# A fused pooled-attention and MLP kernel: q of batch 1 cast by GpSimd's load, w2's last quarters issued sooner, group 0's output units ahead of group 1's hidden pairs

## The chip, the core and the metric

The kernel runs on one core of a Trainium2 chip. A core has five engines with their own instruction streams: TensorE (PE in the profile, with PEld for its weight loads), VectorE (DVE), ScalarE (ACT), GpSimd (POOL) and SyncE (SP), which here only issues transfers. All operands lie in SBUF, a memory of 128 partitions; TensorE writes to PSUM, eight banks of 512 float32 per partition, from which VectorE and ScalarE copy results. Transfers run on 16 DMA engines that the queues share: q1 holds SP's transfers, q10 ScalarE's, q0 GpSimd's. Only GpSimd's queue changes the type of the data on the way.

The metric is the time of one launch on the device in microseconds (us), as the median of several runs.

## What is computed

Eight batches of eight heads, 576 positions, 64 values per head. Keys and values are averaged over blocks of 8 positions (72 pooled positions); each query attends to these. The result, 4608 rows of 512, goes through a two-layer MLP with the gate h - tanh(h).

```python
k_p = k.reshape(B, H, Sp, pool, D).mean(axis=3)      # Sp = 72
v_p = v.reshape(B, H, Sp, pool, D).mean(axis=3)
scores = scale * np.matmul(q, k_p.transpose(0, 1, 3, 2))
attn = softmax(scores)
x = np.matmul(attn, v_p)            # then to (4608, 512)
h = x @ w_in                        # 512 -> 2048
g = h - np.tanh(h)
out = g @ w_out                     # 2048 -> 512
```

## The kernel before

The first 512 positions of each batch b make group b of the MLP (NG = 9 groups of 512 rows; the ninth collects the last 64 positions of all batches). The order of all work is written out by hand, in one program order from which each engine takes its own instructions; the framework adds the waits. While TensorE works on one group's MLP, the other engines load and prepare the next batch.

**Group 0** is special, because attention of batches 0 and 1 and the loads of both weight matrices share its time. `mlp_h_mms` (L577) and `mlp_h_act` (L588, L590) compute its 16 blocks of h. Its output product is made of 16 *units*: `mlp_o(0, tb, qd, gts)` (L605) multiplies row block tb by quarter qd of w2, four matmuls of 512 columns. `W2_ORDER = (0, 8, 4, 12)`: the quarters are the rows 0 to 3, 8 to 11, 4 to 7 and 12 to 15 of w2b, in blocks of 128, each loaded by one `load_w2` (L757) on GpSimd's queue, which casts to 16 bits. The round of units with qd 3 ends with copies into O (L614 by VectorE, L616 by ScalarE) and the stores. The text calls the units of one qd a *round*.

Between the units stands attention of batch 1: pooling of k (`pool_k`, L248 to L259), its transposition (`k_transpose`, L341, with copies into KB on VectorE), the casts of q to 16 bits (`q1_cast` L979, tail L1009), the turn of q by TensorE (`q_pe_transpose` L216, `q_pe_tail` L228, evacuated at L132 or L134), the scores (`scores_wide`, `scores_ends`, L387) and their exponentials on ScalarE (L402, L419, L420), v's pooling (`pool_v1`, L292, L312), the product with v (`av_mms` L476, division L511 and L512) and the turn of the result (`turn1`, L555, evacuated at L562 into xT). These use PSUM banks 4 to 7 in turn, counted by `ps_a`; the units hold banks 0 to 3.

**Groups 1 to 8** use another scheme: seven products of half size in place of eight (one step of Strassen's algorithm in Winograd's form). For it, sums of w2's quarters are prepared once in w2s: `w_sum` (L663) fills w2s[0], [1], [2] on VectorE and w2s[3] on GpSimd, `negated` (L988) fills w2s[4] on ScalarE, and b12 is replaced by b22 - b12 in place. A group's h comes from `h_pair` (L623 on TensorE, tanh at L636 on ScalarE, difference at L637 on VectorE into Gt), seven pairs and two single blocks; VectorE also makes the sums P, Q and the differences Dg (L645, L650, L655). Then follow 14 half products (`product`, L680) with the next batch's scores (`head_scores`, L435) and attention (L461) between them.

In group 1 of the kernel before, one unit of the last round stands behind the second pair (p == 1), and the other three stand in `rest_of_group_0()`, ahead of the fifth pair (p == 4), with the casts and DMA transposes of batch 2's q, the second half of w2s[2], and the difference in b12.

**Loads around the change.** GpSimd issues v of batch 0, four parts of w1, and w2's quarters qd 0 and qd 1 in a row at the start. The quarters qd 2 and 3 are issued after pool_k(1); qd 2 waits until qd 1 has landed, and qd 3 stands behind two parts of w2s[3]. SP issues k of batch 1 (once w1's second part has landed), then q of batch 1 (L172), then v of batch 1 (L138); ScalarE issues the tail of q (L164). A DMA issue also waits for the earlier transfer that had its semaphore.

Of the kernel before, what the change touches and what calls it, by code (L numbers as in the profile page):

```python
# [9 lines left out]
BF16 = mybir.dt.bfloat16  # L10
F16 = mybir.dt.float16
ACT = mybir.ActivationFunctionType
ALU = mybir.AluOpType
# [7 lines left out]
R = 4  # L21
QA = 128 * R
# [7 lines left out]
NT = 5  # L30
# [13 lines left out]
def kernel(  # L44
# [74 lines left out]

    q_raws = {}  # L120
# [104 lines left out]
    def q_pe_tail(b):  # L225
        ps = ps_any([128, NHP, QT], FP32, "qt_ps")
        for hp in range(NHP):
            nc.tensor.matmul(  # L228
                ps[:, hp, :],
                lhsT=q_bf[:, R, 2 * hp : 2 * hp + 2, :].rearrange("p h d -> p (h d)"),  # L230
                rhs=ident[:, 0:QT],
                start=True,
                stop=True,
            )
        evac(q_tiles(b)[1][:, :, :], ps[:, :, :])

    def halves(n, b):
        return ((0, n),) if b < 2 else ((0, n // 2), (n // 2, n))

    def pool_k(b, eng, t0=0, t1=NT, last=None, parts=(0, 1)):  # L240
        r = k_raw[b % 2].rearrange("p t (j d) -> p t j d", d=D)[:, t0:t1, :, :]
        if b not in kdups:
            kdups[b] = work.tile([128, NT, 2, D], BF16, name="kd", tag="kd", bufs=1)
        kd = kdups[b][:, t0:t1, :, :]
        n = t1 - t0
        if 0 in parts:
            for ta, tb in halves(n, b):
                eng.tensor_tensor(  # L248
                    out=r[:, ta:tb, 0:4, :],
                    in0=r[:, ta:tb, 0:4, :],  # L250
                    in1=r[:, ta:tb, 4:8, :],
                    op=ALU.add,
                )
            eng.tensor_tensor(
                out=r[:, :, 0:2, :], in0=r[:, :, 0:2, :], in1=r[:, :, 2:4, :], op=ALU.add
            )
        if 1 not in parts:
            return None
        kd_done = (last or eng).tensor_tensor(  # L259
            out=kd,  # L260
            in0=r[:, :, 0:1, :].to_broadcast([128, n, 2, D]),
            in1=r[:, :, 1:2, :].to_broadcast([128, n, 2, D]),
            op=ALU.add,
        )
        return kd_done
# [489 lines left out]
    def load_w2(i, n):  # L755
        w2_dmas.append(
            nc.gpsimd.dma_start(out=w2b[:, i : i + n, :], in_=w2_src[:, i : i + n, :])  # L757
        )
# [41 lines left out]
    nc.gpsimd.memset(q_bf[64:128, R, :, :], 0.0)  # L800
    nc.gpsimd.memset(mask[:, :, :], 1.0)
# [26 lines left out]
    nc.gpsimd.tensor_copy(out=v_bf[:, NM, :], in_=v_raw[1][:, NM, :])  # L828
    load_w2(8, 4)
# [128 lines left out]
    load_q(1, False)  # L958
    load_main(v_pairs, v_raw[1], 1, 0, 2)
    load_main(v_pairs, v_raw[1], 1, 2, 4)  # L960
    load_q_tail(1, q_raws[1], nc.scalar)
# [16 lines left out]
    def q1_cast(h):  # L978
        nc.scalar.copy(  # L979
            out=q_bf[:, 0:R, h : h + 4, :].rearrange("p j h d -> p h j d"),  # L980
            in_=q1[:, h : h + 4, 0:R, :],
        )

# [9 lines left out]
    q1 = q_raws.pop(1)  # L993
    kd1 = pool_k(1, nc.gpsimd, last=nc.vector)
    load_w2(4, 4)
    after([w2_dmas[2]], w2_dmas[1])
    after([w_sum(w2s[:, 3, :, :], b21, b11, ALU.subtract, nc.gpsimd, k, k + 2) for k in (0, 2)], kd1)
    load_w2(12, 4)
    w_sum(w2s[:, 1, :, :], b11, b12, ALU.add, k1=4)
    mlp_o(0, 0, 0, gts)  # L1000
    q1_cast(0)
    q1_cast(4)
# [3 lines left out]
    mlp_o(0, 3, 0, gts)  # L1006
    mlp_o(0, 0, 1, gts)
    q_pe_transpose(1, (0, 1), "dve")
    nc.scalar.copy(out=q_bf[:QT, R, :, :], in_=q1[:QT, :, R, :])  # L1009
    pool_v1(0, 2)  # L1010
    mlp_o(0, 1, 1, gts)
    scores_wide(1, (0,))
    q_pe_transpose(1, (2,), "act")
    pool_v1(2, 4)
    mlp_o(0, 2, 1, gts)
    scores_wide(1, (1,))
    q_pe_transpose(1, (3,), "act")
    q_pe_tail(1)
    w_sum(w2s[:, 1, :, :], b11, b12, ALU.add, k0=4)
    mlp_o(0, 3, 1, gts)  # L1020
# [3 lines left out]
    w_sum(w2s[:, 2, :, :], b21, b22, ALU.add, k1=4)  # L1024
    w_sum(w2s[:, 0, :, :], b11, b22, ALU.add, k1=4)
    mlp_o(0, 0, 2, gts)
# [6 lines left out]
    w_sum(w2s[:, 0, :, :], b11, b22, ALU.add, k0=4)  # L1033
    mlp_o(0, 1, 2, gts)
    turn1(0)
    mlp_o(0, 2, 2, gts)
    turn1(1)
    av(1, 2, ps_any, True)
    av(1, 3, ps_any, True)
    mlp_o(0, 3, 2, gts)  # L1040
    turn1(2)
    turn1(3)
    av(1, 4, ps_any, True)
    x_pairs.pop((1, 0))
    x_pairs.pop((1, 1))
    x_dma_transpose(1, 2)
    for k in (4, 6):
        w_sum(w2s[:, 3, :, :], b21, b11, ALU.subtract, nc.gpsimd, k, k + 2)
# [7 lines left out]
    def rest_of_group_0():  # L1056
        for n in range(3):
            q_cast_part(2, n)
            q_dma_transpose(2, n)
        for tb in range(1, 4):  # L1060
            mlp_o(0, tb, 3, gts)
        w_sum(w2s[:, 2, :, :], b21, b22, ALU.add, k0=4)
        w_sum(b12, b22, b12, ALU.subtract)
        load_v(3)
        load_q(3)
        v_spread(2, nc.gpsimd)

    for g in range(1, NG):
        nb = g + 1 if g + 1 < B else None
        nn = g + 2 if g + 2 < B else None  # L1070
        for p in range(NP - 1):
            if g == 1 and p == 4:
                rest_of_group_0()
            if nb is not None and g > 1 and p < 3:
                q_cast_part(nb, p)
            h_pair(g, p, ((6, 4, 6, 4, 6, 4, 2) if g == 1 else (0, 2, 4, 6, 0, 2, 4))[p], p % 2)
            if g == 1 and p == 1:
                mlp_o(0, 0, 3, gts)
                negated(1)
# [25 lines left out]
        ps_a = Banks(*((4, 5, 2, 3, 0, 1) if g == 1 else (2, 3, 4, 5, 0, 1)))  # L1105
# [60 lines left out]
```

## Time and profile before

| | us |
|---|---|
| median of 5 runs | 285.64 (285.3 to 285.79) |
| the profiled execution, whole | 285.71 |
| its span, first to last instruction | 284.0 |
| group 0's output product begins | 33.75 |
| group 1's first pair begins | 50.81 |
| group 1's product begins | 68.14 |
| group 2's first pair begins | 83.43 |
| from one group's first pair to the next, group 2 to 3 | 28.8 |
| granted clock of TensorE | 1.00 |

Times in the profile count from the span's start. A row of the timeline gives the start, the length, engine, line, operation, output and input, shapes and count; idle time ahead of it stands in brackets with what ended it. Matmuls are pipelined: one of 512 columns is shown as 0.38 us long, while the next starts 0.216 us later, so rows overlap, and lost time shows best in the distance between starts. The loads before, issue by issue:

```profile
k_raw<-in_k_dram SPq DMA_DIRECT2D x7, 1024.0 KB, 5.9
q_raw<-in_q_dram SPq DMA_DIRECT2D x7, 1024.0 KB, 10.4
w1b<-in_moe_w_in_dram POOLq DMA_DIRECT2D x4, 512.0 KB, 14.2
w2b<-in_moe_w_out_dram POOLq DMA_DIRECT2D x4, 512.0 KB, 15.5
q_raw<-in_q_dram ACTq DMA_DIRECT2D x2, 128.0 KB, 8.1
```

The columns are output and input, the queue, the number of issues, the size of one (counted where it is written) and the median time from issue to landing.

### The profile page before, as it was taken

Reading aid. Unit: us, or ns where it says so; the run is one execution under the profiler, and the core shown is the slowest. Engines: PE = TensorE matmul, PEld = TensorE weight load, DVE = VectorE, ACT = ScalarE, POOL = GpSimd, SP = SyncE. Lnnn points to the kernel's source line nnn. Section 1 sums busy time; section 2 is a strip of 40 time slices with the busy share of each in tenths; the row PEclk is TensorE's granted clock in tenths of the full one; section 3 lists DMA queues with packets and bytes.
Section 4 is the critical chain, followed back from the end, with each engine's and each line's share of the span. In section 5 each row is a group of like instructions: output and inputs, shape, how many; then the busy total and the mean of one; then the engine's idle time right before and its main releaser. Section 6 shows DMA issues by size and latency. Waiting matters only on the chain.

```text
span 284.0 us, 5459 instructions
## 1 busy us (share of the span) xinstructions
PE 275.9 (97%) x2156; PEld 179.8 (63%) x2156; DVE 223.1 (79%) x340; ACT 155.9 (55%) x208; POOL 115.4 (41%) x126
## 2 busy tenths in 40 slices
PE   7899999999999999999999999999999999999994
PEld 2454455645894589448954895479547954884583
DVE  6569889589976997599859995998599839936983
ACT  4737565586527662867186718670868056216610
POOL 8600653992298029901990199009910110010000
PEclk9999999999999999999999999999999999999999
DMA  7999998999947894989588956797640440011014
GB/s 244 233 213 275 282 230 235 313 221 256 295 95 189 270 307 80 162 237 345 103 140 265 336 110 130 226 339 155 115 161 0 76 157 0 2 74 77 0 37 113
DMA packets 66731, 50.41 MB, mean 178 GB/s; under 512 B 42088, under 2 KB 55928, under 8 KB 66706
## 3 DMA queue, kind: packets, MB, share of 16 engines
q1 hardware_dynamic: 57122, 35.96, 49.7%
q0 software_dynamic: 6864, 12.13, 17.3%
q10 hardware_dynamic: 2720, 1.97, 2.4%
q8 instruction: 17, 0.28, 0.4%
q14 instruction: 8, 0.07, 0.1%
HBM read 36.70 MB, written 9.44 MB: 162 GB/s over the span
## 4 chain that ended last, share of the span: by engine, by line
PE 87%; DVE 8%; DMA 2%; ACT 1%; issue 1%; SPq 0%
PE PS L623 37%; PE PS L680 35%; PE PS L577 5%; PE PS L461 3%; PE PS L435 3%; DMA k_raw<-in_k_dram 2%; PE PS L605 2%; DVE Gt L637 2%; DVE w2s L663 1%; DVE v_raw L292 1%; DVE P L645 1%; PE PS L476 1%; DVE x_sb L512 1%; DVE VB L312 0%; DVE qT L134 0%
## 5 line engine op out<-in xcount | busy, mean ns | idle before, releaser
L623 PE MATMUL PS<-xT,w1b 128*128 128x512 bf16 (+1 forms) x504 | 98.3, 355 | 0.0
L637 DVE TENSOR_TENSOR Gt<-PS,TS 128x1024 bf16<-128x1024 f32 x56 | 68.4, 1221 | 34.6 <-ACT TS L636 34.6
L623 PEld LDWEIGHTS <-w1b 128*128 128x128 f16 x576 | 56.3, 98 | 52.7
L636 ACT ACTIVATE TS<-PS 128x1024 f32<-128x1024 f32 x56 | 57.3, 1024 | 31.3 <-PE PS L623 29.8
L724 POOL TENSOR_TENSOR m<-O,m 128x512 f32<-128x512 f32 x6 | 7.6, 1260 | 77.4 <-ACT m L722 77.4
L680 PE MATMUL PS<-w2s,Dg 128*128 128x256 f16 x256 | 30.2, 273 | 0.0
L456 ACT ACTIVATE E<-PS 72x1024 bf16<-72x1024 f32 (+1 forms) x30 | 26.1, 929 | 4.2 <-PE PS L435 4.0
L248 POOL TENSOR_TENSOR k_raw<-k_raw 128x512 f32<-128x512 f32 (+2 forms) x13 | 21.1, 1636 | 17.3 <-DMA k_raw<-in_k_dram 17.3
L680 PEld LDWEIGHTS <-Gt 128*128 128x128 bf16 x256 | 23.6, 98 | 6.8 <-issue 2.3
L680 PEld LDWEIGHTS <-P 128*128 128x128 bf16 x256 | 24.6, 98 | 3.0
L680 PEld LDWEIGHTS <-Dg 128*128 128x128 bf16 x256 | 24.7, 98 | 2.8
L645 DVE TENSOR_TENSOR P<-Gt 128x1024 bf16<-128x1024 bf16 x32 | 22.2, 692 | 0.5
L731 ACT COPY m<-PS 128x512 f32<-128x512 f32 x8 | 4.7, 586 | 29.6 <-PE PS L680 29.6
L696 POOL DMA_DIRECT2D out_dram<-O x14 | 7.7, 551 | 31.7 <-DVE O L734 29.5
L655 DVE TENSOR_TENSOR Dg<-Gt 128x1024 bf16<-128x1024 bf16 x32 | 20.4, 682 | 0.0
L512 DVE TENSOR_TENSOR x_sb<-PS,rden 128x512 bf16<-128x512 f32 x28 | 19.4, 691 | 1.0
L271 POOL TENSOR_TENSOR v_raw<-v_raw 128x512 f32<-128x512 f32 (+1 forms) x12 | 18.2, 1539 | 0.0
L680 PE MATMUL PS<-w2s,Gt 128*128 128x256 f16 x128 | 16.4, 273 | 0.0
L680 PE MATMUL PS<-w2b,P 128*128 128x256 f16 x128 | 16.3, 273 | 0.0
L680 PE MATMUL PS<-w2s,Q 128*128 128x256 f16 x128 | 16.3, 272 | 0.0
L680 PE MATMUL PS<-w2b,Gt 128*128 128x256 f16 x128 | 16.3, 272 | 0.0
L1128 ACT COPY O<-PS 128x512 f32<-128x512 f32 x7 | 4.1, 586 | 21.9 <-PE PS L680 21.9
(121 smaller groups left out, 398.8 us busy)
## 6 DMA issues: line engine op xcount, KB each, us to landing
k_raw<-in_k_dram SPq DMA_DIRECT2D x7, 1024.0 KB, 5.9
q_raw<-in_q_dram SPq DMA_DIRECT2D x7, 1024.0 KB, 10.4
out_dram<-O POOLq DMA_DIRECT2D x14, 512.0 KB, 3.7
v_raw<-in_v_dram SPq DMA_DIRECT2D x6, 1024.0 KB, 7.9
w1b<-in_moe_w_in_dram POOLq DMA_DIRECT2D x4, 512.0 KB, 14.2
w2b<-in_moe_w_out_dram POOLq DMA_DIRECT2D x4, 512.0 KB, 15.5
v_raw<-in_v_dram SPq DMA_DIRECT2D x2, 512.0 KB, 9.7
out_dram<-O SPq DMA_DIRECT2D x2, 512.0 KB, 4.2
```

What stands on the lines that cost most here:

```text
L248: eng.tensor_tensor(out=r[:, ta:tb, 0:4, :], in0=r[:, ta:tb, 0:4, :], in1=r[:, ta:tb, 4:8, :], op=ALU.add,)
L271: eng.tensor_tensor(out=r[:, ta:tb, 0:4, :], in0=r[:, ta:tb, 0:4, :], in1=r[:, ta:tb, 4:8, :], op=ALU.add,)
L435: nc.tensor.matmul(dst, lhsT=kv[a * D : (a + 1) * D, m, :], rhs=rhs, start=True, stop=True,)
L456: nc.scalar.activation(out=e, in_=ps, func=ACT.Exp, scale=SCALE)
L512: nc.vector.tensor_tensor(out=x_sb[:, :, :, :], in0=ps[:, :, :, 0:D], in1=rden[:, :, :, :].to_broadcast([128, 2, 4, D]), op=ALU.mult,)
L577: nc.tensor.matmul(h_tiles[i][:, :], lhsT=w1b[:, fb, i * 128 : (i + 1) * 128], rhs=xT[g][:, :, fb, :], start=(fb == 0), stop=(fb == NFB - 1),)
L623: nc.tensor.matmul(dst[:, t0 * 128 : t1 * 128], lhsT=w1b[:, fb, i * 128 : (i + 1) * 128], rhs=x[:, t0:t1, fb, :], start=(fb == 0), stop=(f ...
L636: nc.scalar.activation(out=t2, in_=PS[:, b0 : b0 + 2, :], func=ACT.Tanh)
L637: nc.vector.tensor_sub(out=Gt[:, p, :, :], in0=PS[:, b0 : b0 + 2, :], in1=t2)
L645: nc.vector.tensor_tensor(out=P[:, a:b, :], in0=Gt[:, a:b, 0, :], in1=Gt[:, a:b, 1, :], op=ALU.add)
L655: return nc.vector.tensor_tensor(out=Dg[:, a:b, :, :], in0=Gt[:, a:b, :, 0:HT], in1=Gt[:, a:b, :, HT:TG], op=ALU.subtract,)
L680: nc.tensor.matmul(part(g, bk, tt), lhsT=lhs(k, slice(tt * 128, (tt + 1) * 128)), rhs=rhs[:, k, :], start=(first and k == 0 and (tt == 0 o ...
```

## The change

- **q of batch 1** is loaded by two DMAs on GpSimd's queue, tail first, that cast it to 16 bits on the way: into the space of w2s[4] and of w2s[3, 6:8], which is free until the w2 sums are made. They stand between w2's first and second quarter. SP's and ScalarE's loads of it go. The rest of the tail's 128 rows is set to zero by a GpSimd memset at the start. What remains of the casts is a copy from head-major to position-major order, half on VectorE, half on ScalarE; the tail is turned straight from where it landed.
- **w2's third and fourth quarter** are issued one after the other behind pool_k(1), with no wait for the second quarter and no GpSimd sums between them. All of GpSimd's sums for w2s[3] come later; the first two wait for v of batch 1 to be placed.
- **The order of group 0's units and of batch 1's attention** is rewritten: all four turns of q, the tail and the first scores stand behind the first round; two units of the second round follow scores, two follow the last scores; all units of the last round stand ahead of group 1's first pair. Group 1's pairs then run without units between them. Batch 2's q casts and DMA transposes are spread over the pairs 3 to 5, the rest of w2s[2] and b12 stand behind pairs 1 and 2, and the PSUM banks of group 1 change accordingly.
- `pool_k` loses a parameter that was not used.

The core of the diff:

```diff
+    q1_bf = (
+        w2s[:, 4, :, :]
+        .rearrange("p a n -> p (a n)")
+        .bitcast(BF16)
+        .rearrange("p (h j d) -> p h j d", h=H, j=R)
+    )
+    q1_tail = (
+        w2s[:, 3, 6:8, :]
...
+    nc.gpsimd.memset(w2s[64:128, 3, 6:8, :], 0.0)
...
     load_w2(0, 4)
     nc.gpsimd.tensor_copy(out=v_bf[:, NM, :], in_=v_raw[1][:, NM, :])
+    nc.gpsimd.dma_start(out=q1_tail[:QT], in_=q[1, :, QA:S, :].rearrange("h p d -> p h d"))
+    nc.gpsimd.dma_start(
+        out=q1_bf, in_=q[1, :, 0:QA, :].rearrange("h (p j) d -> p h j d", j=R)
+    )
     load_w2(8, 4)
...
-    load_q(1, False)
     load_main(v_pairs, v_raw[1], 1, 0, 2)
     load_main(v_pairs, v_raw[1], 1, 2, 4)
-    load_q_tail(1, q_raws[1], nc.scalar)
...
-    kd1 = pool_k(1, nc.gpsimd, last=nc.vector)
+    pool_k(1, nc.gpsimd, last=nc.vector)
     load_w2(4, 4)
-    after([w2_dmas[2]], w2_dmas[1])
-    after([w_sum(w2s[:, 3, :, :], b21, b11, ALU.subtract, nc.gpsimd, k, k + 2) for k in (0, 2)], kd1)
     load_w2(12, 4)
-    w_sum(w2s[:, 1, :, :], b11, b12, ALU.add, k1=4)
+    for h, copy in ((0, nc.vector.tensor_copy), (4, nc.scalar.copy)):
+        copy(
+            out=q_bf[:, 0:R, h : h + 4, :].rearrange("p j h d -> p h j d"),
+            in_=q1_bf[:, h : h + 4, :, :],
+        )
     mlp_o(0, 0, 0, gts)
-    q1_cast(0)
-    q1_cast(4)
     mlp_o(0, 1, 0, gts)
     mlp_o(0, 2, 0, gts)
     k_transpose(1, ps_any, (nc.vector.tensor_copy, nc.vector.tensor_copy))
     mlp_o(0, 3, 0, gts)
+    q_pe_transpose(1, (0, 1), "act")
+    sum1(0)
+    pool_v1(0, 2)
+    q_pe_transpose(1, (2, 3), "act")
+    q_pe_tail(1)
+    scores_wide(1, (0,))
+    placed = pool_v1(2, 4)
     mlp_o(0, 0, 1, gts)
...
+    scores_wide(1, (1,))
     mlp_o(0, 1, 1, gts)
...
     scores_wide(1, (2, 3))
     scores_ends(1)
     negated(0)
...
+    sum2(0)
+    sum0(0)
+    after([w_sum(w2s[:, 3, :, :], b21, b11, ALU.subtract, nc.gpsimd, k, k + 2) for k in (0, 2)], placed)
+    mlp_o(0, 2, 1, gts)
+    mlp_o(0, 3, 1, gts)
...
     av(1, 2, ps_any, True)
     av(1, 3, ps_any, True)
+    negated(1)
+    for k in (4, 6):
+        w_sum(w2s[:, 3, :, :], b21, b11, ALU.subtract, nc.gpsimd, k, k + 2)
+    sum1(4)
+    mlp_o(0, 2, 2, gts)
+    turn1(2)
     mlp_o(0, 3, 2, gts)
-    turn1(2)
     turn1(3)
     av(1, 4, ps_any, True)
+    sum0(4)
+    for tb in range(4):
+        mlp_o(0, tb, 3, gts)
...
-            if g == 1 and p == 4:
-                rest_of_group_0()
+            if g == 1 and 3 <= p < 6:
+                q_cast_part(2, p - 3)
+                q_dma_transpose(2, p - 3)
...
-            h_pair(g, p, ((6, 4, 6, 4, 6, 4, 2) if g == 1 else (0, 2, 4, 6, 0, 2, 4))[p], p % 2)
+            h_pair(g, p, ((6, 4, 2, 6, 0, 2, 4) if g == 1 else (0, 2, 4, 6, 0, 2, 4))[p], p % 2)
             if g == 1 and p == 1:
-                mlp_o(0, 0, 3, gts)
-                negated(1)
+                sum2(4)
+            if g == 1 and p == 2:
+                w_sum(b12, b22, b12, ALU.subtract)
+            if g == 1 and p == 5:
+                load_v(3)
+                load_q(3)
+                v_spread(2, nc.gpsimd)
```

`sum0`, `sum1` and `sum2` are `w_sum` into w2s[0] (b11 + b22), w2s[1] (b11 + b12) and w2s[2] (b21 + b22) for four of the eight k blocks from the argument on.

## The prediction

> **What bounds the kernel now.** I read the shares of busy time first, then the chain of work that ended last, then TensorE's timeline around the change, then the loads. The first two:
>
> ```profile
> PE 275.9 (97%) x2156; PEld 179.8 (63%) x2156; DVE 223.1 (79%) x340; ACT 155.9 (55%) x208; POOL 115.4 (41%) x126
> ...
> PE 87%; DVE 8%; DMA 2%; ACT 1%; issue 1%; SPq 0%
> ```
>
> TensorE sets the time, so the order of its work costs nothing in itself: what counts is where it stands still. The change touches the stretch from group 0's output product (33.75 us) to group 2's start (83.43). TensorE's timeline there:
>
> ```profile
> 43.13 0.43 PE L387 MATMUL PS<-qt,KB 128*32 128x64 bf16 x8
> 43.75 1.02 PE L605 MATMUL PS<-w2b,Gt 128*128 128x512 f16 x4 [0.20 <-DMA w2b<-in_moe_w_out_dram]
> 44.75 0.85 PE L476 MATMUL PS<-VB,E 128*128 128x130 bf16 x12
> 45.44 1.03 PE L605 MATMUL PS<-w2b,Gt 128*128 128x512 f16 x4
> 46.53 0.40 PE L555 MATMUL PS<-ident,x_sb 128*128 128x128 bf16 x4
> ...
> 48.69 0.34 PE L476 MATMUL PS<-VB,E 128*128 128x130 bf16 x3 [0.15 <-ACT xT L562]
> ...
> 49.72 0.90 PE L555 MATMUL PS<-ident,x_sb 128*128 128x128 bf16 x8
> 50.46 0.51 PE L476 MATMUL PS<-VB,E 128*128 128x130 bf16 x6
> ...
> 69.11 0.92 PE L435 MATMUL PS<-qT,KB 64*72 64x512 bf16 x4
> 69.96 1.05 PE L680 MATMUL PS<-w2s,Gt 128*128 128x256 f16 x8
> ...
> 98.23 0.62 PE L435 MATMUL PS<-qT,KB 64*72 64x512 bf16 x4
> 98.78 1.05 PE L680 MATMUL PS<-w2s,Gt 128*128 128x256 f16 x8
> ```
>
> The first column is the start. Four matmuls of 512 columns follow each other in 0.863 us elsewhere (16 of them, 55.20 to 58.65, take 3.45), so a longer step between starts is lost time. 45.44 to 46.53 loses 0.23, 43.75 to 44.75 loses 0.14; eight of 128 columns need 0.45, so 49.72 to 50.46 loses 0.28. The single starts behind these rows give 0.36 ahead of 43.75 (w2's third quarter lands then) and 0.31 ahead of 48.69 (a PSUM bank that ScalarE still empties). In group 1's product the scores step takes 0.85 where group 2's takes 0.55: 0.27 more, since VectorE is late. Together 1.6 us, the most that any order of this stretch can win.
>
> **The change, part by part.** No matmul is added or dropped, so TensorE's own work in the stretch is unchanged. Summed at the rows' pace, from 33.75 on, the new order reaches the first unit of the second w2 quarter (the second round of units) at 38.73 if nothing is late: four units 3.45, the k turn 0.28, the q turns 0.89 and 0.12, one scores step 0.22.
>
> *Stalls that go.* Units of the third round now come after scores, both middle rounds and two attention blocks; the third quarter has 5 us more. The 0.36 goes. The attention blocks get two units between the last exponential and themselves (0.14 goes), the sums ahead of the first divisions come sooner (0.23 goes), and a unit stands between the last two turns (0.28 goes): 1.01 in all. If the third quarter were late again, 0.36 would come back. The 0.31 stays: turn, attention, attention follow each other in the same four banks.
>
> *Loads.* This part decides. Before, q of batch 1 is f32 behind k on SP's queue (q1), its tail on ScalarE's (q10). After, both run on GpSimd's queue (q0), behind w2's first quarter and ahead of its second. v of batch 1 moves up behind k. The queues at 22 to 29 us and 29 to 36 us, and q's arrival:
>
> ```profile
> q0 software_dynamic: 692, 0.69, 58.2%
> q1 hardware_dynamic: 613, 1.18, 50.4%
> q10 hardware_dynamic: 324, 0.08, 5.6%
> ```
>
> ```profile
> q1 hardware_dynamic: 1201, 1.40, 62.0%
> q0 software_dynamic: 598, 0.58, 48.8%
> ```
>
> ```profile
> 36.97 1.99 ACT L979 CAST q_bf<-q_raw 128x1024 bf16<-128x1024 f32 x2 [2.43 <-DMA q_raw<-in_q_dram]
> ```
>
> Columns: packets, MB, share of the 16 engines. Both windows are over 100%, and q0 and q1 move about as many packets when both have work. One packet costs share x window x 16 / packets: q0's (2 KB read, 1 KB written) 94 ns, q1's 58 ns in the second window (mostly q's 1 KB pieces), q10's 256-byte ones 19 ns. No cast of 1 KB pieces is in the trace. From below I take the plain 1 KB row (58), from above the cast row (94); the cast row equals k's plain 2 KB packets (q1 in the first window: 92), so the bytes read set it, and I take 58. The tail's 512 pieces: 19 to 94, taken 25.
>
> The trace's packets show w2's first quarter leaving q0 at 29.6. Then the tail runs beside v: 512 x (25 + 94) / 16 = 3.8 us, to 33.4, by when v is through. Then q alone, 1024 x 58 / 16 = 3.7, to 37.1; then w2's second quarter, 512 x 94 / 16 = 3.0, to 40.1. Consumers start later than the last packet's start: 0.5 us for w2's last quarter (45.88, 46.34), 2.0 for the third (41.73, 43.75), where packets of the next transfer already follow. I take 0.9 as the lower half of this, since the first quarter left somewhat ahead of the pace I use: q usable at 38.0, w2's second quarter at 41.0 less 0.3 for the k transfer, which no longer shares with q10: 40.7.
>
> VectorE's and ScalarE's copies of q follow at 38.0 (ScalarE's row for 1024 elements is 1.04; VectorE's for 1024 16-bit elements 0.69). Behind VectorE's copy on its engine stand the three copies into KB (0.47 + 0.31 + 0.22), which free the banks of the third and fourth q turn; then ScalarE's four evacuations of 0.5 free the banks of the tail and the scores. Chained, the second round starts 2.5 us after q's arrival: 40.5. The quarter, at 40.7, is later. TensorE stands still 40.7 - 38.73 = **1.95 us**, spread over the q turns, scores and the first unit of the second round. By the bounds: with q's pieces at half the plain row (1.9 us) and 0.5 to the consumer the quarter is there at 38.5 (nothing lost); with q and tail at 94 ns it comes 2.3 + 2.2 later (6.4 lost).
>
> One rule speaks against the tail: the Trainium skill, "DMA: Bandwidth & Descriptors", section Specifications, says that below 512 bytes a DMA engine does a read-modify-write and misses line rate. The tail writes 128-byte runs, and no row shows a cast of that size; were each piece twice the 256-byte row, the estimate by that page would put some 0.4 us on top, 287.4.
>
> *Queues passed.* GpSimd gains a memset (0.52, by its q_bf row) ahead of all loads, and two DMA issues (0.97 each by v's row, one perhaps double). It then waits until 30.20 for k anyway. The shift of the loads by up to 0.5 is covered if the DMA engines, busy with k and q of batch 0 until q0's first packet at 8.2, set that start; else it adds 0.5. The last quarter's issue (39.58) no longer stands behind two of GpSimd's w2s[3] differences (2.27); these now wait for batch 1's v. The added wait: ScalarE's second negation stands ahead of two xT evacuations and needs the last quarter, which two quarters of 3.0 and a shared us behind 40.7 put at 47.7; ScalarE comes to it near 48.9, so 1.2 of cover, and each us beyond would hold turn 3. GpSimd's last differences then end at 50.4, so batch 2's k sums start 0.7 later. ScalarE loses one issue (0.62) and two casts. SP's stores of group 0 (1 MB) move ahead of batch 2's transposes; k of batch 2 has 7 us of cover ahead of its head scores, q's transposes some 2 us; gone, that would stall the scores of group 1's product.
>
> *Group 1.* All h pairs now run unbroken, 13.83 us as in group 2. VectorE has beyond group 2's work sum2's second half and the b12 difference:
>
> ```profile
> 62.45 1.25 DVE L663 TENSOR_TENSOR w2s<-w2b 128x1024 f16<-128x1024 f16 x1
> 63.63 1.21 DVE L663 TENSOR_TENSOR w2b<-w2b 128x2048 f16<-128x2048 f16 x1
> 64.76 1.21 DVE L637 TENSOR_TENSOR Gt<-PS,TS 128x1024 bf16<-128x1024 f32 x1
> 65.90 0.67 DVE L645 TENSOR_TENSOR P<-Gt 128x1024 bf16<-128x1024 bf16 x1
> ```
>
> The first takes 1.25 beside GpSimd, 0.69 alone (as at 35.92). Before, the four units of the last round gave VectorE 3.45 us; now only its gaps ahead of the third and fourth Gt do (in group 2 these start 1.55 and 1.72 us after the one before, at 1.14 of work: 0.41 and 0.58). One after the other the two sums take 0.60 (1.18 beside GpSimd) and 1.14, so VectorE enters the fourth Gt 0.75 to 1.3 us later than in group 2, and from there Gt plus P, 1.74, equals TensorE's 1.73 per pair: nothing is made up. In group 2 the last pair's Gt ends 0.82 after the product begins and is wanted at 1.2. So the second scores step waits 0.4 to 1.0; I take 0.65, against 0.27 now: +0.38.
>
> *Sum.* -1.01 + 0.38 + 1.95 = +1.3 us. The profiled execution took 285.71 us (span 284.0 and 1.7 around it), the median is 285.64: 285.7 + 1.3 = **287.0 us**, slower.
>
> **The rivals.** A: *the loads are in time.* Speaking for it: q's casts are half the written bytes, GpSimd issues at some 13 us, and today's q is usable by 36.97; against it: today w2's second quarter leaves q0 at 35.9 without q's 1,536 packets ahead of it. Then -1.01 + 0.38 + 0 to 0.2: 285.1 down to 284.8 with no added VectorE wait. It decides where the second quarter is usable by 39. Faster, 0.25. B: *in between*, a stall of 0.6 to 1.1: 285.1 to 286.2, no change, 0.16. C: *the small casts cost as much as w2's*, 94 ns: the stall grows by 2.3 (q alone) to 4.5 us, 289.3 to 291.5, 0.12. Against it: k's plain 2 KB packets cost the same as w2's casts.
>
> **How the numbers follow.** The forecast (stall of 1.2 to 3.2, 286.2 to 288.3) has 0.47. A measurement here tells 0.2%, 0.57 us, from no change: faster is under 285.07, slower over 286.21. Faster 0.25 (A), same 0.16 (B), slower 0.47 + 0.12 = 0.59. The range goes from 284.9, inside A, to 288.9, short of most of C.
>
> **What would show it.** Right: VectorE and ScalarE wait for the q cast until about 38, and TensorE's first unit of the second round starts near 40.7 on w2's second quarter; no wait for the third or fourth quarter; group 1's pairs 13.8 us in one piece; 0.65 lost at the second scores of its product. From group 2 on nothing moves. Wrong: the second quarter there before 39, q packets on q0 well off 58 ns, h pairs standing still for a bank (two of them are three pairs apart, with 0.4 us of cover for a late Gt), or batch 2's q transposes late.

## The result, and the profile after

| | before | after |
|---|---|---|
| median, all runs of this comparison | 285.56 us (45 runs) | 286.21 us (26 runs) |
| ratio | 1 | 1.0021, 95% interval 1.0013 to 1.0028 |
| the profiled execution, whole | 285.71 | 286.5 |
| group 0's output product begins | 33.75 | 33.25 |
| group 1's first pair begins | 50.81 | 53.95 |
| group 1's product begins | 68.14 | 68.60 |
| group 2's first pair begins | 83.43 | 84.28 |
| from there to the end | 200.56 | 200.50 |

The change costs 0.65 us. From group 2 on nothing moves; the stretch from group 0's product to group 2 grew from 49.68 to 51.03 us. Lines of the changed kernel lie 11 to 16 below those of the kernel before (units L616, h pairs L634, products L691, head scores L446, Gt L648, `w_sum` L674).

Two lines of the page after, busy time and the chain of waits by engine:

```profile
PE 276.3 (97%) x2156; PEld 180.0 (63%) x2156; DVE 224.5 (79%) x339; ACT 155.6 (55%) x208; POOL 119.5 (42%) x129
...
PE 80%; DMA 12%; DVE 5%; POOL 1%; ACT 1%; issue 0%; ACTq 0%; POOLq 0%
```

TensorE's work is the same, but its share of the chain fell from 87% to 80% and the transfers' rose from 2% to 12%: the chain now runs through loads, w2's second quarter (9%) and v of batch 0 ahead of it (3%). TensorE's timeline, early part:

```profile
36.99 1.21 PE L228 MATMUL PS<-ident,q_bf 128*128 128x128 bf16 x16
38.05 0.28 PE L240 MATMUL PS<-ident,w2s 128*128 128x64 bf16 x4
38.53 0.38 PE L398 MATMUL PS<-qT,KB 128*128 128x512 bf16 x1 [0.21 <-ACT qT L144]
39.36 1.02 PE L616 MATMUL PS<-w2b,Gt 128*128 128x512 f16 x4 [0.45 <-DMA w2b<-in_moe_w_out_dram]
...
44.73 1.03 PE L616 MATMUL PS<-w2b,Gt 128*128 128x512 f16 x4
45.64 0.40 PE L566 MATMUL PS<-ident,x_sb 128*128 128x128 bf16 x4
45.88 1.03 PE L616 MATMUL PS<-w2b,Gt 128*128 128x512 f16 x4
46.74 0.39 PE L566 MATMUL PS<-ident,x_sb 128*128 128x128 bf16 x4
...
47.80 0.34 PE L487 MATMUL PS<-VB,E 128*128 128x130 bf16 x3 [0.15 <-ACT xT L573]
```

A unit followed by its successor after 0.86 us has lost nothing. 44.73 to 45.64 loses 0.05 and 45.88 to 46.74 nothing: the four stalls of before are all but gone, and the one of 0.31 at 47.80 is still there. New is the first part. One scores matmul takes 0.22, so 38.53 to 39.36 loses 0.61, on w2's second quarter; ahead of 38.53 stand 0.37 for ScalarE's evacuation of q's turn, and 0.15 within the turns. Together 1.1 us.

TensorE in group 1, and VectorE beside it:

```profile
61.74 4.58 PE L634 MATMUL PS<-xT,w1b 128*128 128x512 bf16 x20
66.88 1.89 PE L634 MATMUL PS<-xT,w1b 128*128 128x512 bf16 x8 [0.56 <-DVE Gt L648]
68.60 1.04 PE L691 MATMUL PS<-w2s,Gt 128*128 128x256 f16 x8
69.57 0.41 PE L446 MATMUL PS<-qT,KB 64*72 64x512 bf16 x2
70.47 0.41 PE L446 MATMUL PS<-qT,KB 64*72 64x512 bf16 x2 [0.50 <-DVE Gt L648]
```

```profile
59.82 1.70 DVE L674 TENSOR_TENSOR w2s<-w2b 128x1024 f16<-128x1024 f16 x1
61.44 1.21 DVE L648 TENSOR_TENSOR Gt<-PS,TS 128x1024 bf16<-128x1024 f32 x1
62.57 1.34 DVE L674 TENSOR_TENSOR w2b<-w2b 128x2048 f16<-128x2048 f16 x1
63.84 1.21 DVE L648 TENSOR_TENSOR Gt<-PS,TS 128x1024 bf16<-128x1024 f32 x1
```

From 61.74, 20 matmuls should take 4.32 and take 5.14 (0.10 and 0.73 lost); from 69.57 two should take 0.22 and take 0.90. TensorE waits 1.51 us for banks that VectorE has yet to read, where the kernel before lost 0.27. VectorE is late because its sum of w2 took 1.70 us. The balance of the stretch by these readings: -0.96 (four stalls of 1.01, of which 0.05 is left) + 1.1 (early) + 1.24 (group 1) = +1.38, against 1.35 measured.

### The profile page after: what moved, and what is told of

Its sections match the earlier page's. It is cut to its first block, busy times and chain, and to the rows that moved or that the text cites. A ratio compares the mean times of both kernels' runs of the same rounds, so it can differ in the third digit from the quotient of the medians.

```text
span 284.8 us, 5459 instructions
## 1 busy us (share of the span) xinstructions
PE 276.3 (97%) x2156; PEld 180.0 (63%) x2156; DVE 224.5 (79%) x339; ACT 155.6 (55%) x208; POOL 119.5 (42%) x129
## 4 chain that ended last, share of the span: by engine, by line
PE 80%; DMA 12%; DVE 5%; POOL 1%; ACT 1%; issue 0%; ACTq 0%; POOLq 0%
PE PS L634 35%; PE PS L691 35%; DMA w2b<-in_moe_w_out_dram 9%; PE PS L616 4%; PE PS L472 3%; PE PS L446 3%; DMA v_raw<-in_v_dram 3%; DVE Gt L648 2%; DVE P L656 1%; DVE w2s L674 1%; PE PS L487 0%; DVE w2b L674 0%; PE PS L398 0%; ACT TS L647 0%; PE PS L566 0%; POOL w2s L842 0%
## 5 line engine op out<-in xcount | busy, mean ns | idle before, releaser
L634 PE MATMUL PS<-xT,w1b 128*128 128x512 bf16 (+1 forms) x504 | 98.2, 355 | 0.6 <-DVE Gt L648 0.6
L648 DVE TENSOR_TENSOR Gt<-PS,TS 128x1024 bf16<-128x1024 f32 x56 | 68.3, 1221 | 33.8 <-ACT TS L647 33.8
L634 PEld LDWEIGHTS <-w1b 128*128 128x128 f16 x576 | 56.4, 98 | 53.6 <-issue 1.1
L647 ACT ACTIVATE TS<-PS 128x1024 f32<-128x1024 f32 x56 | 57.3, 1024 | 30.2 <-PE PS L634 27.4
L691 PE MATMUL PS<-w2s,Dg 128*128 128x256 f16 x256 | 30.2, 272 | 0.0
L691 PEld LDWEIGHTS <-Gt 128*128 128x128 bf16 x256 | 23.6, 98 | 6.8 <-issue 2.3
L691 PEld LDWEIGHTS <-P 128*128 128x128 bf16 x256 | 24.5, 98 | 3.0
L691 PEld LDWEIGHTS <-Dg 128*128 128x128 bf16 x256 | 24.7, 98 | 2.8
L691 PE MATMUL PS<-w2s,Gt 128*128 128x256 f16 x128 | 16.4, 273 | 0.0
L691 PE MATMUL PS<-w2b,P 128*128 128x256 f16 x128 | 16.3, 273 | 0.0
L691 PE MATMUL PS<-w2b,Gt 128*128 128x256 f16 x128 | 16.3, 272 | 0.0
L691 PE MATMUL PS<-w2s,Q 128*128 128x256 f16 x128 | 16.3, 272 | 0.0
```

The costliest lines, as they stand in the source:

```text
L634: nc.tensor.matmul(dst[:, t0 * 128 : t1 * 128], lhsT=w1b[:, fb, i * 128 : (i + 1) * 128], rhs=x[:, t0:t1, fb, :], start=(fb == 0), stop=(f ...
L647: nc.scalar.activation(out=t2, in_=PS[:, b0 : b0 + 2, :], func=ACT.Tanh)
L648: nc.vector.tensor_sub(out=Gt[:, p, :, :], in0=PS[:, b0 : b0 + 2, :], in1=t2)
L691: nc.tensor.matmul(part(g, bk, tt), lhsT=lhs(k, slice(tt * 128, (tt + 1) * 128)), rhs=rhs[:, k, :], start=(first and k == 0 and (tt == 0 o ...
```

## The experiments

All changes are to the changed kernel unless said otherwise. Every profile, whatever its order, ends 200.4 to 200.7 us after group 2's start, so the runs are compared by the *stretch* (group 0's product to group 2's first pair, 49.68 before, 51.03 after) beside their medians. The stretch is of one execution each; the product's start itself lay anywhere from 33.06 to 34.11. By time alone few expectations were met: the theory of e12, the second reading of e11, theory L of e2 and the rivals of e9 and e10. The other medians lie outside every range that was named, so the readings below rest on the traces.

| run | median (runs) | ratio to before, 95% | start | stretch |
|---|---|---|---|---|
| e1 last round back between the pairs | 287.54 (8) | 1.0081, 1.0052 to 1.0110 | 33.13 | 53.69 |
| e2 two sums early | 286.35 (12) | 1.0031, 1.0014 to 1.0048 | 33.06 | 51.33 |
| e3 old load of q, new order | 286.63 (6) | 1.0044, 1.0028 to 1.0060 | 33.24 | 51.86 |
| e4 new load of q, old order | 288.65 (6) | 1.0113, 1.0094 to 1.0131 | 33.62 | 52.96 |
| e5 two sums early, k of batch 3 late | 285.38 (11) | 0.9998, 0.9983 to 1.0013 | 33.54 | 49.48 |
| e6 v behind q | 287.47 (6) | 1.0069, 1.0052 to 1.0086 | 33.59 | 52.40 |
| e7 e5 and e6 | 287.98 (5) | 1.0085, 1.0072 to 1.0099 | 34.11 | 51.41 |
| e8 k of batch 3 late alone | 286.74 (8) | 1.0039, 1.0027 to 1.0052 | 33.36 | 50.96 |
| e9 without two sums of v on GpSimd | 286.04 (10) | 1.0020, 1.0010 to 1.0029 | 33.35 | 50.12 |
| e10 e5, half of v behind q | 285.96 (10) | 1.0025, 1.0004 to 1.0045 | 33.45 | 52.22 |
| e11 e10, both copies of q on VectorE | 285.83 (10) | 1.0027, 0.9998 to 1.0056 | 33.95 | 49.83 |
| e12 e10, q's load in two parts | 285.01 (12) | 0.9982, 0.9959 to 1.0004 | 33.54 | 50.33 |

### Which half of the change: e3 and e4

e3 undoes the load of q and keeps the new order; e4 is the kernel before with nothing but the new load of q.

```diff
# e3 (e4 is the same on the kernel before, the other way round)
-    nc.gpsimd.dma_start(out=q1_tail[:QT], ...)
-    nc.gpsimd.dma_start(out=q1_bf, ...)
...
+    load_q(1, False)
     load_main(v_pairs, v_raw[1], 1, 0, 2)
     load_main(v_pairs, v_raw[1], 1, 2, 4)
+    load_q_tail(1, q_raws[1], nc.scalar)
```

> The changed kernel with the other part undone: q of batch 1 is loaded as before, f32 on SP's queue ahead of v, the tail on ScalarE's, and the copies into q_bf (half VectorE, half ScalarE, tail ScalarE) cast from f32; no zeroing of w2s. Order of units, w2 sums and w2's issues as changed. q should then come near 37 and w2's second quarter by 36.6, as in the kernel before, v some 3 us later than in the changed one. Theory L: the early wait on w2's second quarter (0.61 at the first unit of the second round) goes, but the q turns, which the new order wants 1.3 us earlier than the old one, wait 0.6 longer; together within 0.4 of the changed kernel, 285.8 to 286.6. If the load of q by GpSimd is what costs: 285.1 (the whole 1.1 us back). If the new order needs it: 286.8 or more. Theory V says nothing on the early part and expects its 1.5 us in group 1 unchanged.

> The kernel before with one part of the change alone: q of batch 1 comes through GpSimd's cast load between w2's first and second quarter, its copies into q_bf by ScalarE, the tail turned from where it landed; the order of units, sums and w2's last issues is as before. In this order the first unit of the second quarter is wanted at about 37.0 to 37.5, and the changed kernel's trace has that quarter usable at 39.36. Theory L: TensorE waits about 2 us there, part of it given back since the wait for the third quarter (0.36) moves or goes with its later issue (GpSimd's issue waits for the second quarter's landing): 285.6 + 1.5 to 2.5 = 287.1 to 288.1. If the early wait does not set the time: 285.6 within 0.3.

TensorE's timeline of e3, and of e4, where it comes to w2's second quarter after one round of units:

```profile
39.21 0.38 PE L398 MATMUL PS<-qT,KB 128*128 128x512 bf16 x1 [0.20 <-ACT qT L144]
39.43 1.02 PE L616 MATMUL PS<-w2b,Gt 128*128 128x512 f16 x4
```

```profile
36.49 1.03 PE L619 MATMUL PS<-w2b,Gt 128*128 128x512 f16 x4
39.86 1.02 PE L619 MATMUL PS<-w2b,Gt 128*128 128x512 f16 x4 [2.35 <-DMA w2b<-in_moe_w_out_dram]
```

In e4 four matmuls should take 0.86 and the step is 3.37: 2.5 us lost on the quarter that now stands behind q. The two halves depend on each other: with the old order the new load costs 1.1%, with the new order it takes the ratio from 1.0044 to 1.0021. In e3 TensorE did not wait for the second quarter, but lost 1.2 on the chain of q and k ahead of the second round and 2.1 in group 1. So q's turns and scores ahead of the second round are what makes the new load bearable, and the new order by itself is a loss.

### Who makes VectorE late in group 1: e1, e2, e9

e1 gives VectorE its room back, as in the kernel before; e2 does the two sums ahead of group 1's first Gt; e9 leaves VectorE's order as it is and takes away GpSimd work beside it.

```diff
# e1
-    for tb in range(4):
-        mlp_o(0, tb, 3, gts)
...
+            if g == 1 and p == 4:
+                for tb in range(1, 4):
+                    mlp_o(0, tb, 3, gts)
+                w_sum(b12, b22, b12, ALU.subtract)
...
             if g == 1 and p == 1:
+                mlp_o(0, 0, 3, gts)
# e2
         mlp_o(0, tb, 3, gts)
+    sum2(4)
+    w_sum(b12, b22, b12, ALU.subtract)
...
-            if g == 1 and p == 1:
-                sum2(4)
-            if g == 1 and p == 2:
-                w_sum(b12, b22, b12, ALU.subtract)
# e9
-    pool_v(2, nc.gpsimd, (0, 1))
```

> The changed kernel, with one part undone: the units of the last round stand between group 1's pairs again (one behind the second pair, three ahead of the fifth), with the banks of the kernel before; b12 stands behind them. Theory V (the loss of the change sits in group 1, where VectorE gets no time between the pairs: bank waits of 0.10 and 0.73 and 0.68 at the second scores of the product in the changed kernel's trace, 1.5 us, against 0.27 before): these waits fall to about 0.3, and the time falls by 1.2 us, from 286.2 to about 285.0, below the kernel before (285.6), since the stalls of group 0 that the change takes away stay away. Theory L (the loss is the early wait for q and w2's second quarter, 1.1 us, and VectorE's lag would be made up behind it anyway): no change, 286.0 to 286.4.

> The changed kernel with two VectorE sums moved: the second half of w2s[2] and the difference in b12 leave group 1's pairs and stand behind the copies into O, where VectorE is idle for 2.4 us ahead of the first Gt. Units and loads stay. Theory V: what makes VectorE late are these two sums in the midst of the pairs (1.70 and 1.34 us in the changed kernel's trace), not the missing units as such. In the idle stretch they cost at most 0.7 us of the first Gt, which the gaps of the next two pairs take up; the bank waits go and the second scores lose 0 to 0.3: 286.2 - 1.2 to 1.5 = 284.7 to 285.0. Theory L: no change, 286.0 to 286.4. A third reading (VectorE is late because GpSimd slows all its work) expects the lag to stay at half or more: 285.5 to 285.9.

> The changed kernel without GpSimd's first pooling sums of batch 2's v (batch 2's v is then pooled wrongly by leaving out these two sums; everything else is computed). Theory V (VectorE's sums in group 1 take two to three times their time because GpSimd sums beside them): the sum of w2's second part at 59.8 takes 0.7 to 0.9 us (1.70 in the changed kernel), the one after it 1.15 or less (1.34), and the waits on VectorE inside group 1 (0.10 + 0.73 + 0.68) fall to 0.3 to 0.8 together; time 285.3 to 285.9. Rival (the order alone makes VectorE late, whatever GpSimd does): the sums keep 1.3 to 1.7 us, the waits stay at 1.3 or more, time 286.0 to 286.6.

VectorE's timeline of e9, to set against the rows at 59.82 above:

```profile
59.74 0.68 DVE L674 TENSOR_TENSOR w2s<-w2b 128x1024 f16<-128x1024 f16 x1
60.34 1.22 DVE L648 TENSOR_TENSOR Gt<-PS,TS 128x1024 bf16<-128x1024 f32 x1
61.48 1.22 DVE L674 TENSOR_TENSOR w2b<-w2b 128x2048 f16<-128x2048 f16 x1
62.61 1.22 DVE L648 TENSOR_TENSOR Gt<-PS,TS 128x1024 bf16<-128x1024 f32 x1
```

The same two sums in the same order, and next to no GpSimd work under way when they start (a short copy ends 0.02 us into the second): 0.68 in place of 1.70, and the fourth Gt starts 2.87 us after the first sum in place of 4.02. All waits of 1.51 us for VectorE are gone. It is GpSimd working beside VectorE that makes it late, not the order alone. In e2 the sums lie ahead of group 1 and the waits for VectorE are gone as well; in e1 too.

How late is set by GpSimd's own row. Beside the sum at 59.82 in the changed kernel, and beside the one at 62.45 in the kernel before, GpSimd ran these:

```profile
59.42 1.55 POOL L289 TENSOR_TENSOR v_raw<-v_raw 128x640 f32<-128x640 f32 x1
```

```profile
62.30 0.86 POOL L285 TENSOR_TENSOR vp<-v_raw 128x320 bf16<-128x320 f32 x1
```

They end at 60.97 and 63.16, and VectorE's sums end 0.55 and 0.54 behind them, at 61.52 and 63.70. So do, in all 14 profiles, the sums of this size that start while GpSimd is in such an instruction: each takes what is left of that instruction, and then 0.55 us. (Two that start just as GpSimd goes from one instruction to the next end 0.55 behind the next.)

But the time hardly moves, in e1 it grows. TensorE at the first head scores of group 1's product, in e1, e2 and e9:

```profile
68.13 1.04 PE L691 MATMUL PS<-w2s,Gt 128*128 128x256 f16 x8
71.17 0.62 PE L446 MATMUL PS<-qT,KB 64*72 64x512 bf16 x4 [2.01 <-DMA qT<-q_bf]
```

```profile
67.64 1.04 PE L691 MATMUL PS<-w2s,Gt 128*128 128x256 f16 x8
70.37 0.62 PE L446 MATMUL PS<-qT,KB 64*72 64x512 bf16 x4 [1.69 <-DMA qT<-q_bf]
```

```profile
67.71 1.04 PE L691 MATMUL PS<-w2s,Gt 128*128 128x256 f16 x8
69.45 0.62 PE L446 MATMUL PS<-qT,KB 64*72 64x512 bf16 x4 [0.71 <-DMA qT<-q_bf]
```

Where nothing holds the scores, they start 0.97 after this product does (68.60 and 69.57 in the changed kernel); here they start 3.04, 2.73 and 1.74 after it. Behind the wait for VectorE stood another, for the DMA transposes of batch 2's q, nearly as late. The expectations of e1 and e2 failed on it. e1's profiled execution, the slowest of its eight (289.08), has a second loss, at a lower clock: the granted clock was 0.57 from 71.7 to 75.7 us, and the matmuls there took 1.6 us longer than in e2. No other profile shows this in the stretch, so e1's is too long by about that. Two more of its runs have this profile's mean clock (0.993) and its time; the other five lie between 285.69 and 287.83. In e9 the profiled execution lost 0.77 of the 1.51 it had won; by the ratios (1.0020 against 1.0021) nothing is won. e9's time missed its theory's range; its verdict rests on its trace.

### The wait behind it: e5 and e8

In e2 the transposes are issued at 61.2 and 63.0 and land 6 to 7 us later; ahead of them on SP's queue stands k of batch 3, 1.1 MB, issued at 58.7. e5 is e2 with that load moved behind the transposes; e8 moves it in the changed kernel alone.

```diff
     k_dma_transpose(2)
-    load_k(3)
...
             if g == 1 and p == 5:
+                load_k(3)
                 load_v(3)
```

> The kernel of e2_sums_early (two VectorE sums moved out of group 1's pairs) with the load of batch 3's k moved on SP's queue from ahead of batch 2's q transposes to behind them. In e2 VectorE's lag and the bank waits were gone, but TensorE waited 1.85 us at the first scores of group 1's product for the DMA transposes of batch 2's q, which had 1.1 MB of k ahead of them in the queue. Theory V+T (VectorE's lag is a real cost, and the transposes, late behind that load, are the next wait, nearly as late): the wait falls below 0.4 and the time to 286.2 - 1.5 = 284.5 to 285.0. Rival (the transposes are late of themselves, since ScalarE casts q two pairs later than before): they still land near 69.5 to 70 and the time stays at 285.8 to 286.4.

> The changed kernel with batch 3's k load behind batch 2's q transposes, and nothing else. Theory V+T: VectorE's lag (bank waits 0.83, second scores 0.68) ends last in the changed kernel, the transposes just ahead of it, so nothing is won: 286.0 to 286.4. Rival (the transposes were already what the product waits for): 285.2 or less.

TensorE of e5 at the same place:

```profile
60.80 7.29 PE L634 MATMUL PS<-xT,w1b 128*128 128x512 bf16 x33
67.93 1.04 PE L691 MATMUL PS<-w2s,Gt 128*128 128x256 f16 x8
69.00 0.62 PE L446 MATMUL PS<-qT,KB 64*72 64x512 bf16 x4
```

The pairs run through (33 matmuls in 7.13, which is their pace), and the scores start 1.07 after the product: 0.10 lost. e5 is 0.97 us below e2 and equal to the kernel before (285.38 against 285.52); e8 alone wins nothing. Two causes stood one behind the other; each removed alone gives nothing, both together 0.8 us by the medians (0.7 by the ratios). What made the transposes late is shown only in part: in the kernel before, the same load stood ahead of the same transposes (issued at 58.03 and 60.83) and the scores did not wait for them.

### The early wait: e6, e7, e10, e11, e12

In the changed kernel v of batch 1 on SP's queue shares the DMA engines with q's tail, and w2's second quarter stands behind q. e6 lets v wait until q has landed (and w2's third quarter, and so the fourth behind it, wait for v); e7 adds this to e5; e10 is e5 with only v's second half waiting.

```diff
# e6, e7
-    load_main(v_pairs, v_raw[1], 1, 0, 2)
-    load_main(v_pairs, v_raw[1], 1, 2, 4)
+    v1_dmas = [load_main(v_pairs, v_raw[1], 1, t, t + 2) for t in (0, 2)]
+    after(v1_dmas, q1_dma)
...
     load_w2(4, 4)
+    after([w2_dmas[2]], v1_dmas[1])
# e10
+    after([load_main(v_pairs, v_raw[1], 1, 2, 4)], q1_dma)
# e11: e10, and
-    for h, copy in ((0, nc.vector.tensor_copy), (4, nc.scalar.copy)):
+    for h, copy in ((0, nc.vector.tensor_copy), (4, nc.vector.tensor_copy)):
# e12: e10, and q's load as two of four heads each; v's half waits for the first
+    q1_dma, _ = [
+        nc.gpsimd.dma_start(out=q1_bf[:, h : h + 4], in_=q[1, h : h + 4, 0:QA, :] ...)
+        for h in (0, 4)
+    ]
```

> The changed kernel with two waits added: the loads of batch 1's v start when the cast load of q has landed, and w2's third quarter when v has landed. Theory S (the early stall of 1.1 us comes from v, which moved up and shares the 16 DMA engines with w2's first quarter's end, q and so delays w2's second quarter): alone, q's tail and body need 0.7 + 2.8 us behind 28.8, so q is usable near 33.5 in place of 36.35 and the second quarter near 36.5 to 37.5 in place of 39.36; the early stall falls from 1.1 to 0 to 0.3, and v, usable at 38.5 to 39.5, is just in time. Time 285.1 to 285.5. Rival (v is then late, and the divisions of attention wait for its placing): the stall moves to the attention blocks, 286.0 to 286.8.

> Both together: the two sums early, batch 3's k load behind batch 2's q transposes, v's loads behind q's. If the stall of group 0 and the lag in group 1 are the two separate costs of the change, their gains add: 286.2 - 1.0 - 1.4 = 283.6 to 284.3, below the kernel before by 1.1 to 1.8 us. If a common next wait stands behind both (the transposes of batch 2's q, batch 2's k sums on GpSimd), the gain is that of the better one alone, 284.5 to 285.2.

> The version with the two sums early and k's load of batch 3 late, and besides that only the second half of v's load of batch 1 waits until q's cast load has landed. Theory S (GpSimd's queue with q and w2's second quarter shares the DMA engines with v): q is usable 0.5 to 1 us earlier (36.35 before that), w2's second quarter lands early enough that the second round's first unit waits 0 to 0.2 us for it (0.47), and nothing later gets late, as the second half of v is placed only at 42: 284.6 to 285.2. Rival (as where all of v waited): the load's delay moves on to w2's third quarter, and GpSimd's sums of batch 2's k start 1 us or more later: 285.6 to 286.8.

> As the run before, with both copies of q on VectorE (0.43 us each; ScalarE's took 1.05). If ScalarE's late q copy and evacuations are what the first scores of batch 1 wait for (0.15 + 0.37 us), these waits fall to 0.1 or less and the time by 0.3 to 0.5 more (284.2 to 284.8) where the second quarter is in time; if w2's second quarter is the later of the two, the wait only moves there and the time is within 0.2 of the run before.

> The version with the two sums early and k's load of batch 3 late; q's cast load split in two of four heads each, and the second half of batch 1's v waits for the first of them alone (it waited for the whole of q before, and its sums then started at 41.5 to 43.3, where VectorE has been free from 40.0 on). Theory: v's second half is issued some 1.4 us sooner and its sums start at 40 to 41.7, so that the waits for VB and for the turns of batch 1's x (1.5 + 1.75 us in that profile) go, while w2's second quarter is still in time for the second round (0 to 0.3 us of wait): 284.6 to 285.3, below the kernel before by some 0.5 and with less scatter. Rival (the queues take the time back anyhow: whatever SP's v load is spared later, GpSimd's queue pays earlier): either the second quarter is waited for by 0.4 us or more, or v's sums start after 41.8: 285.3 to 286.3.

In all five the second round starts without a wait for the second quarter. What is late in its place differs. In e6, TensorE at the third round, and VectorE in group 1:

```profile
45.05 1.02 PE L616 MATMUL PS<-w2b,Gt 128*128 128x512 f16 x4 [0.43 <-DMA w2b<-in_moe_w_out_dram]
```

```profile
60.07 2.27 DVE L674 TENSOR_TENSOR w2s<-w2b 128x1024 f16<-128x1024 f16 x1
```

w2's third quarter and k of batch 2 come later, so GpSimd's sums of that k start at 52.5 (49.3 in the changed kernel) and the sum of w2 starts with more of a GpSimd instruction still to run: 2.27 us in place of 1.70, and group 1 loses 2.96 in place of 1.51. e7, where those sums are early, met GpSimd there too: 1.2 and 2.8 us.

In e10 v's second half is late. TensorE of its profiled execution, the slowest of the ten (288.07):

```profile
43.63 0.34 PE L487 MATMUL PS<-VB,E 128*128 128x130 bf16 x3
45.32 0.68 PE L487 MATMUL PS<-VB,E 128*128 128x130 bf16 x9 [1.36 <-DVE VB L323]
45.84 1.03 PE L616 MATMUL PS<-w2b,Gt 128*128 128x512 f16 x4
48.45 0.40 PE L566 MATMUL PS<-ident,x_sb 128*128 128x128 bf16 x4 [1.58 <-DVE x_sb L523]
```

VectorE starts v's sums at 43.3 there, and everything behind them in its order is late too, down to the division whose result TensorE turns at 48.45. In e11's profile (286.08) they start at 41.5, and that division is waited for half as long (0.78 in place of 1.58). e10's ten runs go from 284.79 to 288.07, e11's from 284.58 to 288.94; that the landing of v makes this spread is likely, but only one execution of each was profiled. e11 doesn't show what it was made for: TensorE still loses 0.17 and 0.37 ahead of the scores, so it is the way through turn and evacuation that counts there, not ScalarE's late copy.

e12 issues v's half sooner, and its sums start at 40.4. TensorE of e12's profiled execution, again the slowest of its runs (286.21):

```profile
38.82 0.38 PE L398 MATMUL PS<-qT,KB 128*128 128x512 bf16 x1 [0.21 <-ACT qT L144]
39.03 1.02 PE L616 MATMUL PS<-w2b,Gt 128*128 128x512 f16 x4
...
43.72 0.86 PE L487 MATMUL PS<-VB,E 128*128 128x130 bf16 x12
44.41 1.03 PE L616 MATMUL PS<-w2b,Gt 128*128 128x512 f16 x4
45.49 0.40 PE L566 MATMUL PS<-ident,x_sb 128*128 128x128 bf16 x4
```

No wait for the quarter or for VB of batch 1; 0.37 ahead of the scores as before, 0.22 ahead of the first turn of x (44.41 to 45.49); later in this execution 0.19 and 0.35 for VectorE in group 1, and 0.70 for batch 2's v, which GpSimd's queue spread late. e12's median is 285.01 against 285.37 of the kernel before. That it beats the changed kernel is shown (the intervals lie apart); that it beats the kernel before is likely, but the interval still holds 1.

## Why the prediction was right in direction and wrong in size

**Right.** The sign and the place. Three of the four stalls it named are gone altogether and the fourth down to 0.05; the 0.31 stayed. TensorE waits on w2's second quarter behind q. w2's third and fourth quarter are in time. From group 2 on nothing moves. Rival A (loads in time, 285.1 to 284.8) needed the quarter by 39; it came at 39.36, so rival B (a stall of 0.6 to 1.1) describes the early part better than the forecast did.

**The steps that failed.** Two terms of the sum had the wrong size: the early stall, 1.95, was 1.1, and the wait at the second scores, put at +0.38, was +1.24. They offset each other. A third was put at nothing without a reason: the sum runs from 33.75, as if the product had to start there, and in the changed kernel's profile it starts at 33.25. That 0.5 is what the profiled execution falls short of the forecast (+0.79 in place of +1.3); whether the change causes it is open.

**"TensorE stands still 40.7 - 38.73 = 1.95 us": it was 1.1** (39.36 - 38.23, the product having started 0.5 earlier). The term that failed is "q alone, 1024 x 58 / 16 = 3.7". The queues of the changed kernel from 28.7 to 32.2 us (tail beside v) and from 32.2 to 35.05 us (q alone), columns as in the prediction:

```profile
q1 hardware_dynamic: 535, 1.02, 86.7%
q0 software_dynamic: 539, 0.11, 34.5%
```

```profile
q0 software_dynamic: 1048, 0.54, 137.7%
q1 hardware_dynamic: 35, 0.05, 5.6%
```

By share, a packet of q costs 1.377 x 2.85 x 16 / 1048 = 60 ns, as predicted (58). But the share is 138%: packets on one engine overlap, and these packets, nearly all q's, passed at 2.85 x 16 / 1048 = 44 ns. A share adds up packets in flight; dividing a stretch by its packets gives the pace. Both windows of the prediction were over 100% as well, and it said so without drawing this. The tail and v took 3.4 in place of 3.8, most of w2's first quarter left 0.8 sooner, and from 35.05, when most of q had passed, to the first unit on the second quarter it took 0.7 longer than reckoned: -0.8 - 0.4 - 0.9 + 0.7 = -1.4 on the 40.7.

The tail costs 0.345 x 3.5 x 16 / 539 = 36 ns a packet by share, where the prediction took 25; beside v it did not make the phase longer than predicted. The Trainium skill, "DMA: Bandwidth & Descriptors", section Specifications, has pieces under 512 bytes pay for a read-modify-write. The plain 256-byte row (19) is under 512 bytes as well, so the two rows do not test this, and no run here does; the factor of two in the prediction was its own.

VectorE and ScalarE take q at 36.35, not 38.0; VectorE's copy takes 0.43, ScalarE's 1.05:

```profile
36.35 0.43 DVE L1017 COPY q_bf<-w2s 128x1024 bf16<-128x1024 bf16 x1 [0.80 <-DMA w2s<-in_q_dram]
```

**"So the second scores step waits 0.4 to 1.0; I take 0.65 [...] +0.38": it was 1.51, so +1.24.** The two sums were put at 0.60 (1.18 beside GpSimd) and 1.14, from one row of 1.25. e9 shows the lower end to be right (0.60 and 1.13 from start to start). Beside GpSimd they took 1.62 and 1.27. The prediction read the row of 1.25 as the price beside GpSimd; it is what was left of one GpSimd instruction (0.71) and 0.55, and in the new place 1.15 was left. 0.57 us past the upper end (2.89 against 2.32), VectorE ran out of the cover that the prediction named under what would make it wrong, and pairs stood still for their banks, 0.83 of the 1.51.

**"q's transposes some 2 us" of cover:** none. In e1, e2 and e9, with VectorE's waits gone, TensorE waits 0.8 to 2.1 us for them.

**The sum.** In the stretch the two errors cancel, 0.85 too much early and 0.86 too little in group 1, so +1.35 there is the +1.32 predicted by luck. The time grew by 0.65 only. In the profiled execution the product starts 0.5 sooner than before; 0.3 of this is there already when group 0's h begins, at 18.11 (18.43 before). Among the other profiles the start lies between 33.06 and 34.11, in the old order with the new load at 33.62, so how much of the 0.5 belongs to the change is open; so is how far each median's stretch differs from the one profiled.

## What to carry to other kernels

Before a stall is counted as a gain, look for the wait behind it: here VectorE's sums hid DMA transposes that a load on their queue held up, and only removing both gave time back. A price measured beside another engine can be what was left of that engine's instruction; ask what will be running when the moved work starts in its new place. Where the DMA shares of a stretch add up to over 100%, take packets over time for the pace, not the share. Check that the point from which the sum runs stays where it was.

## What the runs showed of the hardware

VectorE's sum of two 16-bit operands, 128 x 1024, took 0.68 us when no GpSimd instruction ran at its start, and up to 2.32 us (e12) when one did, ending 0.55 behind that instruction or behind the next one (e12); the difference in b12 (128 x 2048) took 1.22, and up to 2.83 (e7), ending 1.08 behind it. Gt, with an operand in PSUM, keeps 1.21 to 1.23 in every profile. GpSimd waits in the same way: its differences for w2s[3] took 1.15 us in the changed kernel beside VectorE's divisions, and 1.52 and 1.60 where they started during a sum of w2 on VectorE.

A cast load that reads 1 KB pieces passed at 44 ns a piece over 16 engines while alone, w2's, which reads 2 KB pieces, at 85 (629 packets in 3.35 us, nearly all w2's, with 288 of SP's beside them).

A DMA transpose of k landed 2.7 to 4.3 us after its issue with no load close ahead of it on SP's queue (2.7 in e2 and e5, 4.3 in the changed kernel), those of q 5.4 to 7.4 us after theirs behind a load of 1.1 MB (changed kernel, e1, e2). They are different transposes, so the comparison is a rough one.
